# Attention with a distance bias and a channel MLP: stores from own tiles, weight casts moved to GpSimd, one load asked for sooner

## The chip, the cores and the metric

The kernel runs on one core of a Trainium2 chip. The core has a matrix engine (TensorE, PE), a vector engine (VectorE, DVE), a scalar engine (ScalarE, ACT), a general engine (GpSimd, POOL) and SyncE (SP), which here issues every DMA. Each has its own queue of instructions, run in order, and they wait for each other by semaphores. The metric is device microseconds of one execution, median of several.

## The reference

Four batches, 8 heads, 576 positions, head width 64, all in float32. Attention with a bias that depends on the distance, then a mixing over positions of rank 32, then a two-layer MLP over channels:

```python
rel = pos[:, None] - pos[None, :]
x = log1p(abs(rel)) / log1p(maximum(pos[:, None], 1))
bias = maximum(x[..., None] @ w1 + b1, 0) @ w2          # 576 x 576 x 8 heads
attn = softmax(q @ k.T / 8 + bias)                      # per batch and head
x = attn @ v                                            # heads side by side: 4 x 576 x 512
u = x + (x.T @ U @ V).T                                 # U 576 x 32, V 32 x 576
out = u + maximum(u @ w_ch1, 0) @ w_ch2                 # 512 -> 2048 -> 512
```

## The kernel before

Stage 1 computes the bias tables (a loop over 36 blocks, ACT, PE and DVE) and writes them to DRAM, from where they are loaded when a pair needs them. It already runs the first score rows of pair 0.

Then come 16 pairs. A pair is two heads of one batch, four pairs to a batch. A pair has 9 slots; `slot(p, s)` issues one block of scores (PE, L310), adds the bias (DVE, L312), takes exponentials (ACT, L331), transposes earlier blocks on PE (`tb`, `ti`, `tm`) and copies them to SBUF (`tr`, `tr_m`, `tr_mid`: "a" is a copy on ACT, L358, "d" one on DVE, L360), and multiplies with v (L414). The previous pair's output is put into `x_sb` by `assemble` (PE transposes L432 and L434, DVE scaling L437, which writes chunks 0 and 1 for the first half and chunks 2 and 3 for the second, and copy of chunk 4, L360). `x_sb` holds one batch: 128 rows by 5 chunks by 512 channels.

Products that need float32 precision are split into a high part (the value rounded by a cast) and a low part (the rest). For q and k `load_part` loads `raw` (one buffer) in two halves per pair, and `prep_ops` makes high (POOL, L142) and low parts (POOL, L150) in four steps, two of them for each half.

After a batch's four pairs its mixing runs inside the next pair, in pairs 5, 9 and 13, and for the last batch within the MLP: `mix_t`, `mix_r`, and then `mix_h` for five chunks in slots 3 (chunk 4), 4 (0 and 1) and 5 (2 and 3). `mix_h` adds a chunk of the mixing to `x_sb` in place (L482) and stores it from there to `u_dram` (L483). In these pairs the first half of the previous pair is assembled at slot 6, the second at slot 8, both into the same `x_sb`.

The MLP weights arrive as int64 words that are converted in the background. The first weight group (of four) is parked in DRAM (`wq_dram`) as float32 and loaded back by `first_weights`, which splits it into high and low parts by `split`: a cast on ACT (L567) and a subtraction on POOL (L568). This happens in pairs 13 to 15, before the MLP begins; `feed` hands it out one step per slot. The MLP then runs over 18 blocks of tokens and four weight groups (first layer L593, second L618).

The order of the work is written by hand: the loops issue the instructions in the order in which each engine will run them, and nothing reorders them. SP's queue is in order too, and a DMA that must wait for its buffer holds up the DMAs behind it.

Of the kernel before, what the change touches and what calls it, by code (L numbers as in the profile page):

```python
# [8 lines left out]
F32 = mybir.dt.float32  # L9
# [5 lines left out]
ALU = mybir.AluOpType  # L15
# [3 lines left out]
B, H, S, D = 4, 8, 576, 64  # L19
HP = H // 2  # L20
DM = H * D
# [4 lines left out]
P = 128  # L26
HALF = S // 2
LEFT = S - 4 * P
K0 = 2 * S + LEFT
QKW = 2 * K0  # L30
# [16 lines left out]
def kernel(  # L47
# [14 lines left out]
    nc = tc.nc  # L62
# [25 lines left out]
    mix = p1.enter_context(tc.tile_pool(name="mix", bufs=1, side="left"))  # L88
# [32 lines left out]
    def load_part(p, a, e):  # L121
        b, hp = divmod(p, HP)
        for lo in (0, D):
            nc.sync.dma_start(out=raw[lo : lo + D, a:e], in_=qk[b, hp, :, a:e])
# [246 lines left out]
    def tr(p, c, hd, eng):  # L371
        hf, o = q_off(c)
        pt = get_pt(p, hf)
        src = pair[p]["P"][c]
        bank = psum("t", [P, 4, P], "tb")
        b0 = 0 if hd == 0 else S + LEFT
        for kb in range(4):
            nc.tensor.transpose(bank[:, kb, :], src[:, b0 + kb * P : b0 + (kb + 1) * P], ident)  # L378
        copy(eng, pt[:, 5 * hd : 5 * hd + 4, o : o + P], bank)
# [98 lines left out]
    def mix_h(b, c):  # L478
        n = P if c < 4 else LEFT
        h = psum("t", [P, DM], "mh")  # L480
        mm(h, lhsT=v4s[:, c * P : (c + 1) * P], rhs=mixt[b], start=True, stop=True)
        nc.vector.tensor_tensor(out=x_sb[0:n, c, :], in0=h[0:n], in1=x_sb[0:n, c, :], op=ALU.add)  # L482
        nc.sync.dma_start(out=u_dram[b * S + c * P : b * S + c * P + n, :], in_=x_sb[0:n, c, :])  # L483

    NP = B * HP

    def slot(p, s):

        new, old = p < NP, p > 0
        if new and (p, s) != (1, 0):  # L490
            scores(p, s)
        if old and s == (AV_OLD if new else AV_LAST):
            av(p - 1, 1)
        if old and s == 0:
            tr(p - 1, 3, 0, "a")
        elif old and s == 1:
            tr(p - 1, 3, 1, "a")
            tr_mid(p - 1, 1, "d")
        elif old and s == (6 if p > HP and p % HP == 1 else 4):
            assemble(p - 1, 0)  # L500
        elif old and s == 8:
            assemble(p - 1, 1)
        if new and 3 <= s <= 8:
            c, hd = divmod(s - 3, 2)
            tr(p, c, hd, "a" if p % HP == 1 and 2 < s < 6 else "da"[hd])
            if s == 5:
                tr_m(p, "a")
            elif s == 6:
                tr_mid(p, 0, "d")
        if new and (p, s) != (1, 0):  # L510
            exps(p, s)
        if s > 0 and new:
            recip(p, s - 1)
        elif s == 0 and old:
            recip(p - 1, 8)
        if new and p > 0 and s == AV_NEW:
            av(p, 0)
# [46 lines left out]
    def split(g, which, k, a, e):  # L564
        def fin(y):
            h, l = (w[:, k, a:e] for w in wq[g][2 * which : 2 * which + 2])
            nc.scalar.copy(out=h, in_=y)  # L567
            nc.gpsimd.tensor_tensor(out=l, in0=y, in1=h.bitcast(F32), op=ALU.subtract)  # L568

        return fin  # L570
# [138 lines left out]
    for i in range(len(order) + 2):  # L709
        if i == 2:  # L710
            nc.vector.tensor_scalar(
                out=tab[:, CUT:NTAB], in0=tab[:, CUT:NTAB], scalar1=w1_sb, scalar2=None, op0=ALU.mult
            )
        if i < len(order):
            bias_hid(order[i])
        if i == len(order) - 1:
            nc.gpsimd.tensor_scalar(
                out=warm, in0=hids[order[i]][3][:, 0:1], scalar1=1.0, scalar2=0.0, op0=ALU.mult, op1=ALU.add
            )
        if i >= 2:  # L720
            bias_mm(order[i - 2])
            bias_out(order[i - 2])
        if i == 9:
            loads += bias_loads(4, 0)
        if i >= 16 and (i - 16) % 8 == 0:
            loads += bias_loads((i - 16) // 8, 0)
        for o in loads[:2]:
            o()
        del loads[:2]
        if 8 <= i < 12:  # L730
            prep.pop(0)()
        if i == 13:
            load_part(1, 0, QKW)
        if i in (20, 26):
            load_v({20: 0, 26: 1}[i])
        if i in early:
            slot(0, early[i])
# [23 lines left out]
    def first_weights(which):  # L761
        ys = []
        for k in range(KD + 2):
            if k < KD:
                ys.append(wrawp.tile([P, CW], I64, tag="wraw", name="y0").bitcast(F32))
                nc.sync.dma_start(out=ys[k], in_=wq_dram[4 * which + k])
            if k >= 2:
                split(0, which, k - 2, 0, DM)(ys[k - 2])
            yield

    feed = iter(())
    for p in range(NP):
        if p > 1:
            new_pair(p)
        if 0 < p < HP - 1:
            bias[p + 1] = big.tile([P, 9 * S], F32, tag=f"big{p + 1}", name=f"bias{p + 1}")
            loads = [o for c in (4, 0, 1, 2, 3) for o in bias_loads(c, p + 1)]
        for s in range(9):
            if s == (1 if p else 0) and p < NP - 1:
                prep = prep_ops(p + 1)  # L780
            if s in ((3, 4, 5, 6) if p else (0, 1, 2, 3)) and p < NP - 1:
                prep.pop(0)()
            if s == 4 and 0 < p < NP - 1:
                load_v(p + 1)
            if s in (6, 8) and 0 < p < NP - 2:
                load_part(p + 2, *((0, K0) if s == 6 else (K0, QKW)))
            if (p, s) == (CONV_FROM[0], 0):
                queue += by_twos(jobs)
                for g in range(4):
                    rows = slice(g * RANK, (g + 1) * RANK)  # L790
                    nc.vector.tensor_copy(
                        fold[rows].rearrange("p (a b) -> p a b", a=4),
                        ident[rows, rows].unsqueeze(1).to_broadcast([RANK, 4, RANK]),
                    )
            if (p, s) == (0, 7):
                av(0, 0)
                new_pair(1)
                scores(1, 0)
                exps(1, 0)
            n = 2 if p else 3  # L800
            for o in loads[0:n]:
                o()
            del loads[0:n]
            if p > 0 or s not in early.values():
                if p > HP and p % HP == 1 and s == 0:
                    mix_t(p // HP - 1)
                slot(p, s)
                conv = (0 if p > HP and p % HP == 1 else 1, 2, 6, 7, 8)
                background(int(s in conv and (p, s) >= CONV_FROM))
            if p > HP and p % HP == 1:  # L810
                if s == 2:
                    mix_r(p // HP - 1)
                for c in {3: (4,), 4: (0, 1), 5: (2, 3)}.get(s, ()):
                    mix_h(p // HP - 1, c)
            if p == NP - 3 and s == 1:
                t = big.tile([P, 9 * S], F32R, tag="big0", name="w1q")
                uth0, *wq[0] = big_views(t, [(4 * LINE, None), (UT, KD), (WQ, KD), (WQ, KD)])
                feed = first_weights(0)
            if p == NP - 2 and s == 1:
                t = big.tile([P, 9 * S], F32R, tag="big1", name="w2q")  # L820
                w2a, w2b, utl0 = big_views(t, [(WQ, KD), (WQ, KD), (UT, KD)])
                wq[0] += [w2a, w2b]
                ut[0] = [(0, uth0)], [(0, utl0)], 0
                feed = first_weights(1)
            if p == NP - 1 and s == 1:
                t = big.tile([P, 9 * S], F32, tag="big2", name="acc")
                acc.update(enumerate(big_views(t, [(DM, 0)] * 10)))
                feed = iter(())
            if p >= NP - 3 and s in (1, 2, 4, 5, 7, 8):
                next(feed, None)  # L830
            if p == NP - 1 and s in (1, 2, 3, 4, 5):
                load_acc(2 * s - 2)
                load_acc(2 * s - 1)
            if p == NP - 1 and s in (6, 7):
                if s == 7:
                    subtract()
                subtract = make_ut(0, s - 6, late=True)
# [3 lines left out]
    def run(*steps):  # L841
        for o in steps:
            o()

    m = [mlp1((0, j, None)) for j in range(3)]
    y = [mlp2((0, j, None)) for j in range(3)]
    slot(NP, 0)
    subtract()
    run(m[0][0])
    t = big.tile([P, 9 * S], F32R, tag="big3", name="ut")  # L850
# [5 lines left out]
    make_ut(1, 0)  # L856
    run(m[0][1])
    slot(NP, 1)
    run(m[0][2])
    make_ut(1, 1)  # L860
    run(m[0][3])
# [152 lines left out]
```

## Time and profile before

| | us |
|---|---|
| median of 3 runs (lowest, highest) | 743.91 (743.39, 745.29) |
| the profiled execution, its own time | 742.59 |
| its span, first to last instruction | 740.5 |
| busy in the span: PE, PEld, DVE, ACT, POOL | 720.5, 579.9, 470.7, 361.3, 241.8 |

PEld is the loading of weights into PE, beside its matmuls. A pair takes from 15.91 to 20.63 us. The page's line on PE in 40 slices of the span reads 8 or 9 tenths busy and above nearly everywhere after the first slices, and PEclk reads 9 in all 40, so that the granted clock never fell. In the rows further down a duration stands behind the start time; "[0.62 <-POOL lo L150]" says that the engine sat idle for 0.62 us before this instruction and that POOL's writing of lo at line 150 ended it. An "xN" behind a row is the number of like instructions that it sums up.

### The profile page before, as it was taken

To read this page: it belongs to the slowest core of one execution; us is meant where nothing else is said; L and a number is where in the kernel's file an instruction comes from. 1 tells how busy PE (TensorE), PEld (TensorE's weight loads), DVE (VectorE), ACT (ScalarE), POOL (GpSimd) and SP (SyncE) were. 2 spreads that over 40 slices of the span, in tenths; PEclk is the share of its full clock that TensorE was granted. 3 is DMA by queue.
4 is the path that set the end of the run, shared out by engine and by line. 5 is a ranking of instruction groups with operands and counts; after the bars stand their busy time and mean duration, and the time that the engine had idled before them with its cause. 6 is when DMAs were issued, how large, how long until landed. Compare 5 with 4: busy or idle time off the path is not lost.

```text
span 740.5 us, 12624 instructions
## 1 busy us (share of the span) xinstructions
PE 720.5 (97%) x4628; PEld 579.9 (78%) x4628; DVE 470.7 (64%) x1018; ACT 361.3 (49%) x807; POOL 241.8 (33%) x256
## 2 busy tenths in 40 slices
PE   6989999999999999999999999999999999999998
PEld 3436888778877887888788888888888888888886
DVE  7995779889978876653447655784456832333343
ACT  7997777878878777862134332440133411011010
POOL 0004567757755657800003333451024500000000
PEclk9999999999999999999999999999999999999999
DMA  7789997475555556500332121230012200001111
GB/s 219 231 306 306 279 276 166 113 204 145 162 165 158 139 139 191 180 27 1 100 135 62 53 72 57 72 100 29 1 42 78 66 0 1 1 28 58 58 42 72
DMA packets 41533, 83.93 MB, mean 113 GB/s; under 512 B 7168, under 2 KB 9856, under 8 KB 41216
## 3 DMA queue, kind: packets, MB, share of 16 engines
q1 hardware_dynamic: 41472, 83.13, 38.0%
q8 instruction: 37, 0.61, 0.4%
q14 instruction: 24, 0.20, 0.1%
HBM read 60.96 MB, written 22.15 MB: 112 GB/s over the span
## 4 chain that ended last, share of the span: by engine, by line
PE 86%; ACT 7%; DMA 3%; DVE 2%; issue 1%; POOL 0%; DVEq 0%; ACTq 0%
PE ph L593 27%; PE po L618 27%; PE o L414 11%; PE sc L310 10%; PE tb L378 7%; ACT ring L235 2%; ACT ring L257 2%; DMA u_dram<-x_sb 1%; ACT p L331 1%; DMA bias_dram<-ring 1%; PE tu L545 1%; PE ti L395 1%; PE bs L246 1%; PE tx L432 1%; PE mt L454 1%
## 5 line engine op out<-in xcount | busy, mean ns | idle before, releaser
L599 DVE SCALAR_TENSOR_TENSOR hh<-ph,hh 128x1024 fp32r<-128x1024 f32 x36 | 44.1, 1224 | 144.6 <-ACT hh L598 144.6
L598 ACT ACTIVATE hh<-ph 128x1024 fp32r<-128x1024 f32 x36 | 37.0, 1027 | 189.9 <-PE ph L593 189.9
L621 DVE TENSOR_TENSOR acc<-po,acc 128x512 f32<-128x512 f32 x132 | 88.4, 684 | 32.3 <-PE po L618 32.2
L201 POOL TENSOR_TENSOR wy<-wt,wy 128x256 int32<-128x256 int32 (+1 forms) x68 | 50.4, 742 | 179.0 <-DVE wt L196 133.5
L331 ACT ACTIVATE p<-p,st 128x576 f32<-128x576 f32 x128 | 100.0, 782 | 6.9 <-DVE st L312 5.8
L618 PE MATMUL po<-w2q,hh 128*128 128x512 f32 x432 | 102.5, 391 | 0.4 <-DVE x_sb L482 0.4
L312 DVE CUSTOM_DVE_ANT_0 p<-sc,bias 128x576 f32<-128x576 f32 x128 | 95.9, 752 | 8.5 <-PE sc L310 6.4
L618 PE MATMUL po<-wq,hh 128*128 128x512 f32 x432 | 100.7, 389 | 0.0
L310 PE MATMUL sc<-hi 128*128 128x288 f32 x320 | 99.6, 329 | 0.0
L618 PEld LDWEIGHTS po<-wq,hh 128*128 128x128 f32 x432 | 81.0, 188 | 16.8
L618 PEld LDWEIGHTS po<-w2q,hh 128*128 128x128 f32 x432 | 80.6, 188 | 17.1 <-ACT ut L548 0.6
L593 PE MATMUL ph<-ut,w1q 128*128 128x512 f32 (+1 forms) x432 | 92.8, 368 | 0.0
L310 PE MATMUL sc<-lo,hi 128*128 128x288 f32 x320 | 89.1, 295 | 0.6 <-POOL lo L150 0.6
L593 PE MATMUL ph<-ut,wq 128*128 128x512 f32 x384 | 89.6, 389 | 0.0
L414 PE MATMUL o<-pt,v 128*64 128x320 f32 (+1 forms) x640 | 85.9, 411 | 0.0
L593 PEld LDWEIGHTS ph<-ut,w1q 128*128 128x128 f32 x432 | 74.7, 188 | 13.7 <-issue 0.6
L593 PEld LDWEIGHTS ph<-ut,wq 128*128 128x128 f32 x384 | 72.1, 188 | 15.0
L378 PE MATMUL tb<-ident,p 128*128 128x128 f32 x512 | 78.1, 275 | 3.9 <-ACT wy L181 1.2
L378 PEld LDWEIGHTS tb<-ident,p 128*128 128x128 f32 x512 | 60.1, 140 | 12.3 <-issue 6.4
L414 PEld LDWEIGHTS o<-pt,v 128*64 128x64 f32 x640 | 48.0, 136 | 27.1 <-issue 3.2
L310 PEld LDWEIGHTS sc<-hi 128*128 128x128 f32 x320 | 60.4, 189 | 9.3 <-issue 3.5
L358 ACT COPY pt<-tb 128x512 f32<-128x512 f32 x88 | 51.2, 582 | 28.1 <-PE tb L378 27.8
(96 smaller groups left out, 1023.3 us busy)
## 6 DMA issues: line engine op xcount, KB each, us to landing
raw<-in_qk_dram SPq DMA_DIRECT2D x56, 304.0 KB, 5.1
wraw<-in_w_ch_dram SPq DMA_DIRECT2D x64, 256.0 KB, 2.7
bias_dram<-ring SPq DMA_DIRECT2D x36, 288.0 KB, 3.9
v<-in_vp_dram SPq DMA_DIRECT2D x16, 320.0 KB, 3.7
bias<-bias_dram SPq DMA_DIRECT2D x16, 288.0 KB, 5.0
acc<-u_dram SPq DMA_DIRECT2D x18, 256.0 KB, 4.9
out_dram<-acc SPq DMA_DIRECT2D x18, 256.0 KB, 2.0
bias<-bias_dram SPq DMA_DIRECT2D x16, 256.0 KB, 5.6
```

What stands on the lines that cost most here:

```text
L201: nc.gpsimd.tensor_tensor(out=st["y"], in0=st["t"], in1=st["y"], op=ALU.add)
L310: mm(ps[:, a, 0:HALF], lhsT=hi[:, q0 : q0 + P], rhs=kk, start=(i == 0), stop=(i == n - 1))
L312: nc.vector.tensor_tensor_reduce(out=halves(dst), in0=ps[:, :, 0:HALF], in1=halves(bias[hp][:, s * S : (s + 1) * S]), scale=-0.125, scalar ...
L331: nc.scalar.activation(out=dst, in_=dst, func=AF.Exp, bias=st[:, s : s + 1], scale=-1.0, accum_out=st[:, 10 + s : 11 + s])
L358: nc.scalar.copy(out=out, in_=in_)
L378: nc.tensor.transpose(bank[:, kb, :], src[:, b0 + kb * P : b0 + (kb + 1) * P], ident)
L414: mm(o[hd * D : (hd + 1) * D, 0:n], lhsT=v[:, vb * D : (vb + 1) * D], rhs=pt[:, pb, :], start=(j == 0), stop=(j == 4),)
L593: mm(st["ps"][:, f, :], lhsT=w, rhs=x, start=(i == 0), stop=(i == 3 * KD - 1))
L598: nc.scalar.activation(out=hh[u], in_=st["ps"], func=AF.Relu)
L599: nc.vector.scalar_tensor_tensor(out=hl[u], in0=st["ps"], scalar=0.0, in1=hh[u].bitcast(F32), op0=ALU.max, op1=ALU.subtract)
L618: mm(ps, lhsT=h, rhs=w, start=(m == 0), stop=(m == 3 * nf - 1))
L621: nc.vector.tensor_tensor(out=a, in0=ps, in1=a, op=ALU.add)
```

## The change

Five edits. First, `mix_h` writes chunks 0 and 1 into tiles of their own (u0, u1) and stores them from there; chunks 2 to 4 stay as they were. Second, in pair 1 the copies of pt in slots 3 to 5 go to DVE and ACT in turn, as in an ordinary pair, where they all went to ACT. Third, pair 1's q and k are loaded in two halves in stage 1, at blocks 13 and 17, where one load at block 13 had fetched both. Fourth, pair 4's halves are asked for in slots 4 and 6 of pair 2 instead of 6 and 8. Fifth, `first_weights` no longer uses `split`: its cast is a POOL instruction like L142, in front of POOL's subtraction. Both weight sets are now fed in pair 14 (slots 1, 2, 4, 7), pair 15 (slots 1, 2, 3, 4, 5, 7) and after the first two closing slots, where they were fed in pairs 13 to 15.

```diff
@@ mix_h
-        nc.vector.tensor_tensor(out=x_sb[0:n, c, :], in0=h[0:n], in1=x_sb[0:n, c, :], op=ALU.add)
-        nc.sync.dma_start(out=u_dram[b * S + c * P : b * S + c * P + n, :], in_=x_sb[0:n, c, :])
+        u = mix.tile([P, DM], F32, tag=f"u{c}", name="u") if c < 2 else x_sb[:, c, :]
+        nc.vector.tensor_tensor(out=u[0:n], in0=h[0:n], in1=x_sb[0:n, c, :], op=ALU.add)
+        nc.sync.dma_start(out=u_dram[b * S + c * P : b * S + c * P + n, :], in_=u[0:n])
@@ slot
-            tr(p, c, hd, "a" if p % HP == 1 and 2 < s < 6 else "da"[hd])
+            tr(p, c, hd, "a" if p > HP and p % HP == 1 and 2 < s < 6 else "da"[hd])
@@ stage 1
-        if i == 13:
-            load_part(1, 0, QKW)
+        if i in (13, 17):
+            load_part(1, *((0, K0) if i == 13 else (K0, QKW)))
@@ first_weights
-                split(0, which, k - 2, 0, DM)(ys[k - 2])
+                h, l = (w[:, k - 2] for w in wq[0][2 * which : 2 * which + 2])
+                nc.gpsimd.tensor_scalar(
+                    out=h, in0=ys[k - 2], scalar1=1.0, scalar2=0.0, op0=ALU.mult, op1=ALU.add
+                )
+                nc.gpsimd.tensor_tensor(out=l, in0=ys[k - 2], in1=h.bitcast(F32), op=ALU.subtract)
@@ the loop of the pairs
-            if s in (6, 8) and 0 < p < NP - 2:
-                load_part(p + 2, *((0, K0) if s == 6 else (K0, QKW)))
+            at = (4, 6) if p == 2 else (6, 8)
+            if s in at and 0 < p < NP - 2:
+                load_part(p + 2, *((0, K0) if s == at[0] else (K0, QKW)))
...
-                feed = first_weights(0)
...
-                feed = first_weights(1)
+                feed = (None for which in range(2) for _ in first_weights(which))
...
-                feed = iter(())
-            if p >= NP - 3 and s in (1, 2, 4, 5, 7, 8):
+            if s in {NP - 2: (1, 2, 4, 7), NP - 1: (1, 2, 3, 4, 5, 7)}.get(p, ()):
                 next(feed, None)
@@ the closing slots
     slot(NP, 0)
+    next(feed)
...
     slot(NP, 1)
+    next(feed)
```

On SP, in pair 2, slots 4 to 8, the order before is this (bias_1102 is the bias of pair 3, raw the halves of pair 4's q and k, wraw words to be converted):

```order
L129 DMA v<-in_vp_dram 128x640
L274 DMA bias_1102<-bias_dram 128x576
L274 DMA bias_1102<-bias_dram 128x512
L274 DMA bias_1102<-bias_dram 128x64
L274 DMA bias_1102<-bias_dram 128x576
L124 DMA raw<-in_qk_dram 64x1216 x2
L274 DMA bias_1102<-bias_dram 128x512
L274 DMA bias_1102<-bias_dram 128x64
L171 DMA wraw<-in_v_dram 128x256
L124 DMA raw<-in_qk_dram 64x1216 x2
```

And now, with the same bias under the name bias_1104:

```order
L129 DMA v<-in_vp_dram 128x640
L124 DMA raw<-in_qk_dram 64x1216 x2
L274 DMA bias_1104<-bias_dram 128x576
L274 DMA bias_1104<-bias_dram 128x512
L274 DMA bias_1104<-bias_dram 128x64
L274 DMA bias_1104<-bias_dram 128x576
L124 DMA raw<-in_qk_dram 64x1216 x2
L274 DMA bias_1104<-bias_dram 128x512
L274 DMA bias_1104<-bias_dram 128x64
L171 DMA wraw<-in_v_dram 128x256
```

The first half of raw has moved past four bias loads, the second past two more and past the load of wraw.

On POOL, in pair 14, from behind the pm of that pair to the pm of pair 15, before (hi and lo are pair 15's q and k, w2q the second-layer weights):

```order
L142 TENSOR_SCALAR hi<-raw 128x1216
L150 TENSOR_TENSOR hi<-raw,hi 64x608 x2
L568 TENSOR_TENSOR w2q<-y_3902,w2q 128x512
L142 TENSOR_SCALAR hi<-raw 128x1216
L568 TENSOR_TENSOR w2q<-y_3911,w2q 128x512
L150 TENSOR_TENSOR lo<-raw,hi 128x608 x2
L568 TENSOR_TENSOR w2q<-y_3965,w2q 128x512
L568 TENSOR_TENSOR w2q<-y_3991,w2q 128x512
L351 TENSOR_SCALAR pm<-praw,st 128x576
```

And now (w1q the first-layer weights, which before had their turn in pair 13 and at the start of pair 14):

```order
L142 TENSOR_SCALAR hi<-raw 128x1216
L150 TENSOR_TENSOR hi<-raw,hi 64x608 x2
L770 TENSOR_SCALAR w1q<-y_3894 128x512
L773 TENSOR_TENSOR w1q<-y_3894,w1q 128x512
L142 TENSOR_SCALAR hi<-raw 128x1216
L150 TENSOR_TENSOR lo<-raw,hi 128x608 x2
L770 TENSOR_SCALAR w1q<-y_3903 128x512
L773 TENSOR_TENSOR w1q<-y_3903,w1q 128x512
L351 TENSOR_SCALAR pm<-praw,st 128x576
```

Before the last two low parts of pair 15's k stood two subtractions, and now a cast and a subtraction; behind them there were two subtractions, now a cast and a subtraction.

On ACT, in pair 14, slots 4 to 8, before (L331 exponentials, L358 copies of transposed blocks):

```order
L358 COPY pt<-tb 128x4x128
L331 ACTIVATE p,st<-p,st 128x576
L567 CAST w2q<-y_3902 128x512
L358 COPY pt<-tm 128x4x64 x2
L331 ACTIVATE p,st<-p,st 128x576
L567 CAST w2q<-y_3911 128x512
L358 COPY pt<-tb 128x4x128
L331 ACTIVATE p,st<-p,st 128x576 x2
L567 CAST w2q<-y_3965 128x512
L358 COPY pt<-tb 128x4x128
L331 ACTIVATE p,st<-p,st 128x576
```

And now:

```order
L358 COPY pt<-tb 128x4x128
L331 ACTIVATE p,st<-p,st 128x576
L358 COPY pt<-tm 128x4x64 x2
L331 ACTIVATE p,st<-p,st 128x576
L358 COPY pt<-tb 128x4x128
L331 ACTIVATE p,st<-p,st 128x576 x2
L358 COPY pt<-tb 128x4x128
L331 ACTIVATE p,st<-p,st 128x576
```

The casts are gone, and nothing has come in their place.

## Rows read from the trace of the kernel before

**Rows 1.** The page, part 1: busy us (share of the span) xinstructions of each engine.

```profile
PE 720.5 (97%) x4628; PEld 579.9 (78%) x4628; DVE 470.7 (64%) x1018; ACT 361.3 (49%) x807; POOL 241.8 (33%) x256
```

**Rows 2.** Windows: us; busy us of PE, PEld, DVE, ACT, POOL; PEclk; DMA; GB/s.

```profile
116.65:133.47 16.82, 16.20 (x127) 13.54 (x127) 15.19 (x37) 13.36 (x36) 14.02 (x15) 1.00 0.51 133
133.47:153.72 20.25, 19.54 (x151) 14.66 (x150) 17.16 (x40) 15.03 (x38) 15.37 (x15) 1.00 0.62 168
153.72:169.63 15.91, 15.91 (x128) 13.49 (x127) 13.41 (x39) 13.11 (x34) 8.59 (x9) 1.00 0.61 159
201.44:221.89 20.45, 19.28 (x150) 14.69 (x150) 16.72 (x42) 15.21 (x38) 13.30 (x12) 1.00 0.61 175
269.65:290.28 20.63, 19.35 (x150) 14.70 (x149) 13.74 (x36) 14.57 (x36) 13.39 (x12) 1.00 0.60 181
290.28:307.02 16.74, 16.36 (x128) 13.55 (x127) 11.49 (x34) 13.96 (x35) 12.16 (x11) 1.00 0.58 150
414.78:740.50 325.72, 322.14 (x1489) 269.37 (x1487) 163.42 (x267) 71.16 (x149) 60.72 (x83) 1.00 0.14 46
```

**Rows 3.** Timeline of stage 1: start, us, engine, line, out<-in, [idle before <-releaser].

```profile
37.87 0.76 DVE L312 CUSTOM_DVE_ANT_0 p<-sc,bias 128x576 f32<-128x576 f32 x1 [0.70 <-DMA bias<-bias_dram]
...
38.67 0.78 ACT L331 ACTIVATE p<-p,st 128x576 f32<-128x576 f32 x1 [0.26 <-DVE st L312]
```

**Rows 4.** Timeline around pair 4's first scores; last row: the tile bias, 60 to 126 us.

```profile
103.75 1.08 SPq L274 DMA_DIRECT2D bias<-bias_dram  x2
...
116.42 1.21 POOL L142 TENSOR_SCALAR hi<-raw 128x1216 fp32r<-128x1216 f32 x1 [0.93 <-DMA raw<-in_qk_dram]
...
117.70 3.02 POOL L150 TENSOR_TENSOR lo<-raw,hi 128x608 fp32r<-128x608 f32 x2
...
116.72 0.75 DVE L312 CUSTOM_DVE_ANT_0 p<-sc,bias 128x576 f32<-128x576 f32 x1
...
120.78 0.40 PE L310 MATMUL sc<-lo,hi 128*128 128x288 f32 x1 [0.62 <-POOL lo L150]
...
DMA to landing us min/median/max: 2.9/5.3/8.8
```

**Rows 5.** Timeline of the mix pairs 5, 9, 13; last row: the waits of DVE.

```profile
152.37 0.44 PE L432 MATMUL tx<-ident,ot 128*128 128x128 f32 x2 [0.35 <-DVE x_sb L360]
...
153.16 0.63 PE L378 MATMUL tb<-ident,p 128*128 128x128 f32 x4 [0.35 <-DVE pt L360]
...
151.64 0.42 DVE L437 TENSOR_TENSOR x_sb<-tx,st 128x256 f32<-128x256 f32 x1 [1.22 <-DMA u_dram<-x_sb]
...
220.14 0.63 PE L378 MATMUL tb<-ident,p 128*128 128x128 f32 x4 [1.17 <-ACT wy L181]
...
288.55 0.63 PE L378 MATMUL tb<-ident,p 128*128 128x128 f32 x4 [0.98 <-DVE x_sb L360]
...
DVE x_sb L437 <- DMA u_dram<-x_sb: 3.2, 3, 1.2
```

**Rows 6.** Timeline of pair 13, ACT and PE.

```profile
283.75 0.61 ACT L567 CAST w1q<-y 128x512 fp32r<-128x512 f32 x1
...
284.90 0.51 PE L481 MATMUL mh<-ts,v4s 128*128 128x512 f32 x1 [0.30 <-ACT pt L358]
```

**Rows 7.** Timeline of pair 14, ACT and PE.

```profile
304.50 0.62 ACT L567 CAST w2q<-y 128x512 fp32r<-128x512 f32 x1
...
306.43 0.66 PE L378 MATMUL tb<-ident,p 128*128 128x128 f32 x4 [0.36 <-ACT p L331]
```

**Rows 8.** Timeline of POOL in pairs 14 and 15, and PE's first second-layer matmuls.

```profile
303.43 1.29 POOL L568 TENSOR_TENSOR w2q<-y,w2q 128x512 fp32r<-128x512 f32 x1 [1.21 <-issue]
...
307.10 2.93 POOL L150 TENSOR_TENSOR lo<-raw,hi 128x608 fp32r<-128x608 f32 x2
...
313.71 1.04 POOL L351 TENSOR_SCALAR pm<-praw,st 128x576 f32<-128x576 f32 x2 [1.19 <-DVE st L343]
...
344.59 5.64 PE L618 MATMUL po<-w2q,hh 128*128 128x512 f32 x24
```

## The prediction, made before the changed kernel was run

> **What bounds the kernel now.** I read the page's busy shares first. TensorE (PE) is busy for 720.5 of 740.5 us, 97% [rows 1]. No other engine is near that, so an edit to VectorE (DVE), ScalarE (ACT), GpSimd (POOL) or the DMA queue is worth only the time in which PE waits for it. The change alters no matmul: PE can win back idle time and nothing else.
>
> Next I read the windows [rows 2]. The granted clock is 1.00 in every one, the 2.4 GHz level, so no stage has a clock to win or lose. From 414.78 us to the end PE is busy for 322.14 of 325.72 us, and there the edits move nothing. The pairs are different. I cut them at the 20 value matmuls with which every pair begins. Pair 6 (153.72 to 169.63) is one without a wait: 15.91 us, PE busy 15.91. Against it stand pair 4 (16.82) and pair 14 (16.74) with the same matmuls. Pairs 5, 9 and 13 also carry a batch's mixing, and take 20.25, 20.45 and 20.63 us with PE busy for 19.54, 19.28 and 19.35. Their PE work is one and the same, so the smallest busy time, 19.28, is the most that such a pair can need.
>
> Last I read the timelines for what each of these waits is for. Pair 4: PE's score matmul at 120.78 sat idle 0.62 us for POOL's low parts of k, which were late because POOL's cast before them had sat 0.93 us for the DMA of raw [rows 4]. Mix pairs: PE's transposes sat idle 0.35 and 0.35 us in pair 5, 1.17 in pair 9 and 0.98 in pair 13. DVE's assembly of x_sb (L437) had sat for the store of x_sb to u_dram, three times, 3.2 us in all, 1.22 of it in pair 5 [rows 5]. The page calls the 1.17 a wait for ACT's L181; DVE's wait, of almost that size and right before it, is the cause I go by. Pair 13 loses 0.30 us more behind a copy of pt on ACT, which stood behind a weight cast of 0.61 us [rows 6]. Pair 14: 0.36 us behind an exponential on ACT, with a cast of 0.62 us shortly before it [rows 7].
>
> **The change part by part.**
>
> *Own tiles for the mixed chunks 0 and 1.* L437 at slot 6 writes x_sb[:, 0:2]. It no longer has to wait until the stores of these chunks land. Nothing is added: same five additions on DVE, same five stores on SP. Behind L437 on DVE are the copies that PE's next transposes need, so DVE's wait goes straight to PE. By the windows pair 5 gains 20.25 - 19.28 = 0.97 [rows 2]. For pair 9 the same gives 1.17, but DVE's waits in pairs 9 and 13 together are 3.2 - 1.22 = 2.0, about 1.0 each [rows 5]; I take 1.0. For pair 13 I take PE's idle time in front of this wait, 0.98. Together 2.95. Lower bound: pair 5 by its recorded idle of 0.70, and half of the rest if the next wait (chunks 2 and 3, which stay in x_sb) comes up: 1.7. Upper: 0.97 + 1.17 + 1.35 = 3.5, of which 0.3 is the next part's.
>
> *The casts leave ACT.* Eight ACT casts of about 0.61 us go, four in pair 13 and the start of 14, four in pair 14 and the start of 15. PE gains the 0.30 of pair 13 [rows 6] and, in pair 14, 16.74 - 15.91 = 0.83 [rows 2], of which only 0.36 stands in one idle row [rows 7]: the rest lies in matmuls that start a little late each. Together 1.13, bounds 0.66 and 1.2.
>
> The Trainium skill ("Perfetto Trace Analysis", Identifying the Most-Contended Engine) calls matmul busy time a poor measure of nearness to the limit, since matmuls are pipelined. This trace agrees: pair 14 shows 16.36 busy for work that takes 15.91 in pair 6 [rows 2]. By idle rows alone the change would win 4.1, by periods 5.2.
>
> POOL takes eight casts over, and before did only the subtraction, 1.29 us [rows 8]. No row shows a POOL cast of 128x512. The nearest is the same instruction over 128x1216, 1.21 us [rows 4], by elements 1.21 x 512/1216 = 0.51. Bounds: nothing below the 0.51 is in reach, and 1.21 if size did not matter; I take 0.51. The cover: in pair 14 the order is now one cast and one subtraction ahead of the low parts of pair 15's k, 0.51 + 1.29 = 1.80, where two subtractions stood, 2.58. So these low parts (307.10 before) come 0.8 us sooner; at 1.21 for the cast it is 2.50 against 2.58, still no later. POOL is busy 12.16 of 16.74 us there [rows 2], has 1.21 us idle before a subtraction, and 1.19 before the pm of pair 15 [rows 8]. After pm (over at 314.75) come six cast-and-subtract steps, 6 x 1.80 = 10.8, done by 325.6 if nothing else holds them; the second-layer weights are first read by PE at 344.59 [rows 8]. Cost to PE: 0, at either bound.
>
> The Trainium skill ("Perfetto Trace Analysis", Optimizing GPSIMD Operations) speaks against this part: other engines are to be preferred, GpSimd being slower in general. Per element these rows show the reverse for this cast, 0.51 against 0.62, as an estimate. By the rule the work would take longer, and whether anything waits for it is the third rival.
>
> *Pair 4's q and k asked for two slots sooner.* A slot is 15.91/9 = 1.77 us, so both halves are asked for 3.5 us sooner; POOL's wait was 0.93. POOL's low parts ended at 117.70 + 3.02 = 120.72 and would now end at 119.79; PE would want them at 120.78 - 0.62 = 120.16 [rows 4]. The stall goes, 0.4 us to spare. By the windows 16.82 - 15.91 = 0.91, by the idle row 0.62; I take 0.91. The price lies on SP, which issues in order: the last bias loads of pair 3 are now behind both halves. They were issued at 103.75, landing 2.9 to 8.8 us after issue, and DVE uses the bias at 116.72. Two more issues cost about 1.08, as two do there; 104.83 + 8.8 = 113.6 leaves 3.1 us for the extra bytes ahead. I take no cost; if the bytes took longer, DVE would wait up to the 0.91 gained.
>
> *Pair 1.* Its load in two halves at i = 13 and 17 puts half of the bytes in front of stage 1's bias loads. DVE sat 0.70 us for one of these, and ACT 0.26 for DVE [rows 3]. ACT sets the pace in stage 1, so 0.26 is the gain, bounds -0.3 (the second half now holds a later bias load as long) and 0.26. Two copies of pt per pair 1 go from ACT to DVE; I see no row in which PE idles for them and take 0, bounds -0.2 and 0.2.
>
> Sum: 2.95 + 1.13 + 0.91 + 0.26 = 5.25 us. The profiled execution took 742.59 (span 740.5 and 2.09 around it), which would become 737.3. The median of the runs shown is 743.91, 1.32 higher, and goes to 738.7. Every part of it lies ahead of 414.78, and from there on PE is the bound, so what PE gains it keeps.
>
> **The rivals.**
>
> *The next wait takes over.* In the mix pairs DVE is busy for 17.16 of 20.25 and 16.72 of 20.45 us [rows 2]; with its wait gone it has 2 to 3 us left, and the second half of x_sb still waits for stores of its own. And pair 3's bias may eat pair 4's gain. For it: the densest DVE windows of all the pairs are these. Against it: pair 13 with 13.74 busy shows the same loss as the other two, so it is the wait and not DVE's load. Then half of 2.95 and the 0.91 are lost, 2.4 in all: 741.1.
>
> *The transfers were hidden anyway.* The waits at u_dram and raw go, but PE is as late for another reason (a PSUM bank, ACT's L181, which the page names for the 1.17). Then only ACT's relief and stage 1 are left, 1.13 + 0.26 = 1.4: 742.5. Against it: idle times and waits agree in size in four places.
>
> *POOL becomes the bound, and the kernel slower.* Let a POOL cast take c. The low parts of pair 15's k are ahead of its own scores; they would be late by (c + 1.29) - 2.58 = c - 1.29, at the most, and PE with them. After pm the six steps take 6(c + 1.29), and 344.59 - 314.75 = 29.84 us are there, so from c = 3.7 on PE waits for the second-layer weights too, with 6 us for each us of c. The gain is used up at (c - 1.29) + 6(c - 3.7) = 5.25, so c = 4.1; at c = 4.5 the kernel takes 743.91 - 5.25 + 3.2 + 4.8 = 746.7. For it speaks that no row shows this shape on POOL; against it that the same instruction over 2.4 times the elements takes 1.21.
>
> **How the numbers follow.** The forecast, about 738.7, has a chance of 0.68; its own range is 738.1 to 740.1: at the upper bounds 3.5 + 0.9 + 0.91 + 0.46 = 5.8 is gained, and by idle rows alone 4.1, less 0.3 if stage 1 loses, 3.8. The next wait takes over: 0.18, at about 741.1. Hidden anyway: 0.10, at 742.5. POOL the bound: 0.04, at 746.7. About 0.3%, 2.2 us, is what a measurement of this kernel can tell from no change, so faster means below 741.7. Faster: all of the forecast and of the first rival, 0.86. Same: 0.10. Slower: 0.04. The range, 737.0 to 741.4, takes in the forecast with its bounds, 1.1 below it for the spread of the runs, which is 743.39 to 745.29 now, and most of the first rival; about 0.18 is left out.
>
> **What would show it.** DVE's wait of L437 for the store of u_dram is gone in all three mix pairs, and these take 19.3 to 19.6 us. Pair 4 takes 15.9, PE has no wait for POOL's lo near 120 us, and DVE none for a bias of pair 3 near 116. No cast of w1q or w2q is on ACT before the weights of the second group, and pair 14 takes 15.9. POOL's cast of 128x512 takes about 0.5 us. I am wrong where the mix pairs stay at 20 us with the wait gone, where DVE shows a new wait for bias, or where PE waits for POOL at the first lines of the MLP (L594, L619 of the changed kernel).

## The result, and the profile after

The changed kernel takes 738.29 us (median of 5, 736.59 to 740.56); the kernel before, timed beside it, 744.61 (743.39 to 745.94). The ratio is 0.9914 with a 95% interval of 0.9887 to 0.994. The prediction was 738.7, within 737.0 to 741.4. The profiled execution took 736.59, its span is 734.8 against 740.5.

The page's first part, and the windows cut at the same places as [rows 2], with pairs 3 and 15 in addition (us; busy us of PE, PEld, DVE, ACT, POOL; PEclk; DMA share; GB/s):

```profile
PE 719.6 (98%) x4628; PEld 580.4 (79%) x4628; DVE 471.5 (64%) x1020; ACT 356.3 (48%) x797; POOL 246.8 (34%) x264
```

```profile
99.86:115.75 15.89, 15.89 (x127) 13.35 (x127) 13.48 (x37) 12.04 (x31) 9.97 (x11) 1.00 1.06 267
115.75:131.90 16.15, 16.15 (x127) 13.50 (x127) 14.53 (x37) 14.12 (x38) 13.36 (x15) 1.00 0.63 154
131.90:151.03 19.13, 19.13 (x151) 14.68 (x150) 17.30 (x42) 15.08 (x39) 15.33 (x15) 1.00 0.59 170
151.03:166.95 15.92, 15.92 (x127) 13.56 (x126) 13.17 (x37) 13.05 (x34) 8.64 (x10) 1.00 0.67 168
198.75:218.12 19.37, 19.30 (x151) 14.70 (x150) 16.64 (x42) 14.95 (x38) 13.35 (x12) 1.00 0.61 173
265.88:285.26 19.38, 19.31 (x151) 14.72 (x150) 13.58 (x36) 13.65 (x34) 11.81 (x10) 1.00 0.47 136
285.26:301.18 15.92, 15.92 (x127) 13.56 (x127) 10.74 (x31) 11.75 (x30) 8.87 (x9) 1.00 0.58 154
301.18:318.72 17.54, 17.21 (x136) 14.18 (x135) 12.00 (x35) 13.05 (x33) 14.33 (x16) 1.00 0.65 214
409.00:734.80 325.80, 322.04 (x1489) 269.27 (x1487) 163.28 (x267) 71.14 (x148) 60.55 (x83) 1.00 0.14 46
```

From above: pair 3 takes 15.89 us, at a DMA share of 1.06; pair 4 16.15 (16.82 before), pair 5 19.13 (20.25), pair 6 15.92 (15.91), pair 9 19.37 (20.45), pair 13 19.38 (20.63), pair 14 15.92 (16.74), pair 15 17.54, as before. PE's busy time has hardly changed, 719.6 against 720.5: 5.7 us of span went, nearly all of it idle time or time in which matmuls started late. The last window is as long as before, 325.80 against 325.72.

All waits of PE that the view still lists (us in all, times, the longest):

```profile
PE bs L246 <- ACT ring L235: 7.3, 6, 5.3
PE bs L246 <- ACT ring L257: 1.1, 1, 1.1
PE tb L378 <- ACT p L331: 0.8, 1, 0.8
PE po L619 <- DVE x_sb L483: 0.4, 1, 0.4
PE tx L432 <- DVE pt L360: 0.2, 1, 0.2
PE tb L378 <- DVE w2q L554: 0.2, 1, 0.2
```

Of the PE waits in [rows 4 to 7] none is left. DVE's wait for the store, 3.2 us in three times before [rows 5], now stands once:

```profile
DVE x_sb L437 <- DMA u_dram<-x_sb: 0.2, 1, 0.2
```

Not everything that stood in front of them went as forecast. This is the timeline around pair 4's first scores, which answers to [rows 4]:

```profile
103.73 0.30 PE L310 MATMUL sc<-lo,hi 128*128 128x288 f32 x1
...
104.16 0.76 DVE L312 CUSTOM_DVE_ANT_0 praw<-sc,bias 128x576 f32<-128x576 f32 x1 [1.74 <-DMA v<-in_vp_dram]
...
114.88 1.21 POOL L142 TENSOR_SCALAR hi<-raw 128x1216 fp32r<-128x1216 f32 x1 [0.97 <-DMA raw<-in_qk_dram]
...
116.17 3.01 POOL L150 TENSOR_TENSOR lo<-raw,hi 128x608 fp32r<-128x608 f32 x2
...
116.21 0.45 ACT L178 ACTIVATE wt<-wraw 128x256 f32<-128x256 f32 x1 [1.16 <-DMA wraw<-in_v_dram]
...
119.23 0.40 PE L310 MATMUL sc<-lo,hi 128*128 128x288 f32 x1
```

POOL still waits 0.97 us for raw, and ACT has a new wait of 1.16 for words of in_v. PE's row at 119.23 bears no wait: POOL ended at 119.18, just in time.

DVE's 1.74 at 104.16, in front of its row for pair 3's first scores, looks like a new DMA wait, but the name misleads. The last of the score matmuls that this row reads starts at 103.73, 0.43 us earlier. In the kernel before, the same row stands 0.43 us behind the same matmul (104.64), and there the wait is put down to PE:

```profile
105.07 0.76 DVE L312 CUSTOM_DVE_ANT_0 praw<-sc,bias 128x576 f32<-128x576 f32 x1 [2.40 <-PE sc L310]
```

It is 0.43 us in all fourteen profiles of this document, so the wait is for PE's scores in each. The bias that the row reads was asked for ahead of raw, in slot 0 of pair 2.

POOL in pairs 14 and 15, and PE's first second-layer matmuls, which answer to [rows 8]:

```profile
297.31 0.62 POOL L770 TENSOR_SCALAR w1q<-y 128x512 fp32r<-128x512 f32 x1
...
298.01 1.29 POOL L773 TENSOR_TENSOR w1q<-y,w1q 128x512 fp32r<-128x512 f32 x1
...
300.55 2.95 POOL L150 TENSOR_TENSOR lo<-raw,hi 128x608 fp32r<-128x608 f32 x2
...
319.70 1.28 POOL L773 TENSOR_TENSOR w2q<-y,w2q 128x512 fp32r<-128x512 f32 x1
...
338.75 5.64 PE L619 MATMUL po<-w2q,hh 128*128 128x512 f32 x24
```

A cast lasts 0.62 us, and its subtraction starts 0.70 us after the cast's start. The last split ends at 320.98, almost 18 us before its first reader.

### The profile page after: what moved, and what is told of

Same layout as the page of the kernel before. It is cut to its first block, busy times and chain, and to the rows that moved or that the text cites. A ratio compares the mean times of both kernels' runs of the same rounds, so it can differ in the third digit from the quotient of the medians.

```text
span 734.8 us, 12632 instructions
## 1 busy us (share of the span) xinstructions
PE 719.6 (98%) x4628; PEld 580.4 (79%) x4628; DVE 471.5 (64%) x1020; ACT 356.3 (48%) x797; POOL 246.8 (34%) x264
## 4 chain that ended last, share of the span: by engine, by line
PE 91%; ACT 5%; issue 2%; DVE 1%; DMA 0%; ACTq 0%; DVEq 0%
PE ph L594 27%; PE po L619 27%; PE sc L310 11%; PE o L414 11%; PE tb L378 8%; ACT ring L235 2%; PE bs L246 1%; ACT ring L257 1%; PE tm L386 1%; PE tx L432 1%; PE ti L395 1%; PE tu L546 1%; PE mh L481 1%; PE mt L454 1%; ACT p L331 1%
## 5 line engine op out<-in xcount | busy, mean ns | idle before, releaser
L331 ACT ACTIVATE p<-p,st 128x576 f32<-128x576 f32 x128 | 100.0, 782 | 4.1 <-DVE st L312 2.9
L358 ACT COPY pt<-tb 128x512 f32<-128x512 f32 x86 | 49.9, 581 | 28.6 <-PE tb L378 28.3
```

Source lines behind the costliest of these rows:

```text
L331: nc.scalar.activation(out=dst, in_=dst, func=AF.Exp, bias=st[:, s : s + 1], scale=-1.0, accum_out=st[:, 10 + s : 11 + s])
L358: nc.scalar.copy(out=out, in_=in_)
```

## The experiments

In all of them a pair is cut at the first of its 20 value matmuls, as in [rows 2]; "pairs 3 and 4" is the time from pair 3's cut to pair 5's, "stage 1" the time up to pair 1's cut (64.47 us before, 63.83 after).

**1. The own tiles alone.** On the kernel before:

```diff
+        u = mix.tile([P, DM], F32, tag=f"u{c}", name="u") if c < 2 else x_sb[:, c, :]
-        nc.vector.tensor_tensor(out=x_sb[0:n, c, :], in0=h[0:n], in1=x_sb[0:n, c, :], op=ALU.add)
+        nc.vector.tensor_tensor(out=u[0:n], in0=h[0:n], in1=x_sb[0:n, c, :], op=ALU.add)
```

> The kernel before with the own tiles for mixed chunks 0 and 1 alone. Theory A (each edit takes away a PE wait of its own, and the gains add up): DVE's wait of L437 for u_dram goes in all three mix pairs; pair 5 falls from 20.25 to about 19.15 us, pair 9 from 20.45 to 19.4, pair 13 from 20.63 to about 19.65 (its 0.30 behind the ACT cast stays); all other pairs as before; about 3.1 us less in all. Theory B (the gain of the mix pairs needs the other edits, since ACT's casts or a later wait would take over): half of that or less, pair 13 above 20.1.

Ratio 0.9958 (0.994 to 0.9976), median 740.52. Windows of pairs 5, 9 and 13:

```profile
134.85:153.99 19.14, 19.14 (x150) 14.69 (x149) 17.27 (x42) 15.11 (x39) 15.33 (x15) 1.00 0.59 169
201.73:221.10 19.37, 19.28 (x151) 14.69 (x150) 16.64 (x42) 15.23 (x38) 13.33 (x12) 1.00 0.59 175
268.86:288.43 19.57, 19.26 (x151) 14.68 (x150) 13.65 (x36) 14.58 (x36) 12.37 (x11) 1.00 0.59 170
```

The mix pairs gain 1.11, 1.08 and 1.06 us, 3.25 in all, without any other edit: theory A. In the three profiles of experiments 2 to 4, which lack this edit, they take 20.08 to 20.24, 20.40 to 20.53 and 20.51 to 20.61 us, so the gain is clear of what differs between executions. One thing was not expected: pair 4, in which nothing was changed, takes 18.32 us instead of 16.82.

**2. The split on GpSimd alone.** The edits to `first_weights` and to the feed's times, on the kernel before.

> The kernel before with the first MLP weights split on GpSimd in pairs 14 and 15 alone. Theory A: pair 14 falls from 16.74 to 15.92 us and pair 13 from 20.63 to about 20.33; pair 15 stays at 17.54; 1.1 us less in all. Theory B: in pair 13 the wait for the store of x_sb comes last, so ACT's 0.30 us there is hidden behind it: pair 13 stays within 0.1 of 20.63, and 0.8 us less in all.

Ratio 0.9985 (0.9957 to 1.0012), median 743.38. Pairs 13 and 14:

```profile
270.22:290.73 20.51, 19.27 (x150) 14.68 (x150) 13.66 (x36) 13.66 (x34) 11.85 (x10) 1.00 0.50 146
290.73:306.66 15.93, 15.93 (x128) 13.59 (x127) 10.68 (x31) 11.78 (x30) 8.89 (x9) 1.00 0.49 133
```

Pair 14 falls by the 0.81 us. Pair 13, at 20.51, stays within 0.12 of before (it takes 20.53 in experiment 4, which doesn't touch it): theory B. ACT's 0.30 us [rows 6] is hidden behind the store while that is waited for. With the own tiles, pair 13 goes from 19.57 (experiment 1) to 19.38, so the two together give 0.19 more.

**3. Pair 4's load alone.**

```diff
+            at = (4, 6) if p == 2 else (6, 8)
-            if s in (6, 8) and 0 < p < NP - 2:
-                load_part(p + 2, *((0, K0) if s == 6 else (K0, QKW)))
+            if s in at and 0 < p < NP - 2:
+                load_part(p + 2, *((0, K0) if s == at[0] else (K0, QKW)))
```

> The kernel before with pair 4's q and k asked for two slots sooner, alone. Theory A: pair 4 falls from 16.82 to about 16.15 us, as in the changed kernel, with 0.7 us less in all, and DVE gets a wait of 1 to 2 us for pair 3's bias near 104 us that PE does not feel. Theory B (the DMA queue is full there, and the load lands no sooner; what moved pair 4 in the changed kernel was the shift of the work before it): pair 4 stays above 16.6.

Ratio 1.0007 (0.9989 to 1.0025), median 744.34: no gain shows. Pair 4 took 17.45 us. Two rows of DVE and ACT in pair 4:

```profile
118.67 0.76 DVE L312 CUSTOM_DVE_ANT_0 p<-sc,bias 128x576 f32<-128x576 f32 x1 [0.55 <-DMA bias<-bias_dram]
...
120.13 0.45 ACT L178 ACTIVATE wt<-wraw 128x256 f32<-128x256 f32 x1 [2.84 <-DMA wraw<-in_v_dram]
```

ACT stands 2.84 us for words that were asked for behind raw, DVE 0.55 for the last part of pair 3's bias. The price that the prediction set at nothing is there. The wait near 104 us that theory A speaks of is the misread one: here that row, at 106.39, waits 2.17 us for PE's scores.

**4. Stage 1 and pair 1 alone.** The load of pair 1 in halves and the shared copies.

> The kernel before with pair 1's load in two halves and pair 1's copies shared with DVE, alone. Theory A: stage 1, up to the first value matmul of pair 1 at 64.47 us, ends 0.26 us sooner by the load (64.2), the rest of the 0.64 us seen in the changed kernel being a start that differs from run to run (PE's second group at 18.82 against 18.40); pair 1 falls from 20.39 to about 20.11 by the copies; 0.5 us less in all. Theory B: all of the 0.64 comes from the load: 63.85, with PE's second group at 18.8.

Ratio 0.9985 (0.9963 to 1.0007), median 742.11. Pair 1 and pair 4:

```profile
63.79:83.90 20.11, 19.25 (x144) 15.16 (x143) 12.32 (x37) 13.69 (x35) 10.97 (x10) 1.00 1.01 265
```

Pair 4, not edited here, is another draw: 17.65. Pair 1 falls from 20.39 to 20.11. It does so in every profile with these two edits (20.10 to 20.13, one of 20.48) and in none without them (20.37 to 20.39). That is 0.27 us; I put it down to the copies, since the load was issued by 34 us and POOL takes it up at 59 without a wait, but no run separates the two.

Stage 1 ended at 63.79, as in theory B. Over all profiles it ended at 63.75 to 64.79 with the edit (ten) and at 64.34, 64.45, 64.47 and 65.82 without (four): its start differs too much to compare ends. DVE's wait for a bias in stage 1 stands in all four (0.64 to 1.68 us) and in none of the ten. What it is worth can be read from a row of PE just before it, which every profile has, and PE's next wait behind it. In the kernel before:

```profile
35.25 1.18 PE L246 MATMUL bs<-ring,small_sb 128*32 128x288 f32 x16 [0.68 <-ACT ring L235]
...
41.79 2.47 PE L246 MATMUL bs<-ring,small_sb 128*32 128x288 f32 x32 [1.42 <-ACT ring L257]
```

And in the changed kernel:

```profile
34.97 1.18 PE L246 MATMUL bs<-ring,small_sb 128*32 128x288 f32 x16 [0.68 <-ACT ring L235]
...
41.14 2.47 PE L246 MATMUL bs<-ring,small_sb 128*32 128x288 f32 x32 [1.05 <-ACT ring L257]
```

From the start of the first of these rows to pair 1's cut pass 28.84 to 28.87 us in all ten profiles with the edit, and 29.16, 29.20 and 29.22 in three without it. The load in halves is worth 0.34 us, and the rest of the 0.64 is the start: theory A. The fourth without it has 30.46, with a slower clock (last section).

**5. The casts back on ACT, at the new times.**

```diff
-                nc.gpsimd.tensor_scalar(out=h, in0=ys[k - 2], scalar1=1.0, scalar2=0.0, ...)
-                nc.gpsimd.tensor_tensor(out=l, in0=ys[k - 2], in1=h.bitcast(F32), op=ALU.subtract)
+                split(0, which, k - 2, 0, DM)(ys[k - 2])
```

> The changed kernel, but with the casts of the first MLP weights left on ACT at their new times (pairs 14 and 15, closing slots). Theory A (what helps is that ACT is relieved): pair 13 stays at 19.4 us, since nothing is cast there any more; pair 14 takes 16.2 to 16.7 instead of 15.92, pair 15 17.8 to 18.4 instead of 17.54; 0.5 to 1.5 us more than the changed kernel. Theory B (what helps is the new time alone): pair 14 at 15.92, pair 15 at 17.54. Pair 4, which has the sooner load here, gives one more sample of it: 16.2 to 17.5.

Ratio 0.9922 (0.9894 to 0.995), median 738.73. Pairs 14 and 15:

```profile
285.64:301.86 16.22, 16.20 (x128) 13.54 (x127) 11.04 (x32) 12.38 (x32) 8.14 (x8) 1.00 0.55 144
301.86:319.50 17.64, 17.25 (x135) 14.18 (x135) 11.78 (x34) 14.78 (x38) 8.64 (x9) 1.00 0.66 210
```

Against the changed kernel 0.30 and 0.10 us, 0.4 in all. Moving the work out of pair 13 and thinning it out in pair 14 gives most of the gain (0.6 of the 1.0 us that pairs 13 to 15 win beside the own tiles), taking it off ACT the rest. Both theories hold a part.

**6. GpSimd's casts at the old times.** The feed as before, the casts as in the changed kernel.

> The changed kernel, but with the first MLP weights fed at the old times (pairs 13 to 15), cast on GpSimd. Theory A (the new times are needed because GpSimd would be too late for pair 15's k): two cast-and-subtract steps of 0.70 + 1.28 stand ahead of pair 15's low parts, these end near 305.4 us where PE wants them near 304.25, so pair 15 takes 18.5 instead of 17.54, with a PE wait for POOL; pairs 13 and 14 as in the changed kernel. Theory B (GpSimd has room enough anyway): all pairs as in the changed kernel. Pair 4: 16.2 to 17.5.

Ratio 0.9921 (0.9898 to 0.9944), median 739.27. Pair 15 takes 18.47 us, with this row of PE:

```profile
305.93 0.40 PE L310 MATMUL sc<-lo,hi 128*128 128x288 f32 x1 [0.64 <-POOL lo L150]
```

As theory A had it, 18.5: two splits ahead of pair 15's low parts are one too many.

**7. Every GpSimd cast four times over.**

```diff
+                for _ in range(4):
                     nc.gpsimd.tensor_scalar(...)
```

> The changed kernel with each GpSimd cast of the first MLP weights made four times over (same result), so that a cast costs about 2.8 us instead of 0.70. Theory A (the sum of the third rival): pair 15's low parts end 2.1 us later, at 305.6, against 0.75 us of slack, so pair 15 takes 18.9 instead of 17.54 with a PE wait for POOL; the first and second layers of the MLP wait for nothing; 1.3 us more in all. Theory B (GpSimd's work is covered more deeply, or less): pair 15 within 0.3 of 17.54, or over 20, or a wait for POOL at the first lines of the MLP. Pair 4: 16.2 to 17.5.

Ratio 0.9928 (0.9903 to 0.9952), median 739.69. Pair 15 takes 18.75 us instead of 17.54, with one wait for POOL, and the MLP waits for nothing:

```profile
310.62 0.40 PE L310 MATMUL sc<-lo,hi 128*128 128x288 f32 x1 [0.90 <-POOL lo L150]
```

1.21 us against 1.35 worked out. The third rival's own sum gives 2.8 - 1.29 = 1.5 us "at the most", and that holds: a cast of 2.8 us costs 1.21 here, and the kernel would still have been faster. Pairs 3 and 4 took 36.55 us, with the same instructions as the changed kernel's 32.04.

**8. The changed kernel without pair 4's sooner load.** The edit of experiment 3 undone.

> The changed kernel without the sooner load of pair 4's q and k. Theory A (the load is worth 0.7 us on the average, under a spread of about 1 us that the DMA queue brings): pair 4 takes 16.8 to 18.3 us as in the four profiles without the sooner load so far (16.82, 18.32, 17.34, 17.65). Theory B (the load is worth nothing; pair 4 is short when the DMAs of pairs 1 to 3 happen to land early): pair 4 within 16.1 to 17.5. A single profile tells little here; it is read together with the other three of this set, which have the sooner load.

Ratio 0.9937 (0.9912 to 0.9961), median 740.03 (738.39 to 744.44). Pair 4 took 19.61 us. All profiles together, but for experiments 10 to 12, which change more: pairs 3 and 4 took 32.70, 33.24, 34.02, 34.22 and 36.15 us without the sooner load, 31.83, 32.04, 32.41, 33.34, 35.50 and 36.55 with it. The means, 34.07 and 33.61, are closer than the spread. The medians speak for the load (740.03 against 738.29 and, below, 738.25), but come from different runs. What this edit is worth stays open.

What it shifts is clearer. PE's listed waits for POOL's low parts in these pairs sum to 0, 0, 0.3, 0.3, 1.7 and 2.6 us with the sooner load, and to 0.6, 1.0, 1.4, 1.9 and 2.0 without. ACT's first conversion of the words behind raw starts after 1.16 to 4.77 us of idle time in all six with it, and without a wait in all five without it. DVE waits for the last part of pair 3's bias in three of the six (0.55, 2.14 and 3.10 us) and in none of the five.

**9. The changed kernel once more.** The same program.

> The changed kernel once more, for a second profile of the same program and more times. Theory A (the spread of pairs 3 and 4 is the DMA queue's and differs from execution to execution): everything from pair 5 on as in the first profile within 0.1 us a pair, pairs 3 and 4 together anywhere between 31.8 and 36.5 us, stage 1 between 63.7 and 64.7. Theory B (the first profile's 32.04 is the program's own): within 0.3 of it. The ratio to the kernel before about 0.992.

Ratio 0.9905 (0.9889 to 0.9921), median 738.25 (736.66 to 741.08). The profiled execution is the longest of the six, 741.08. From pair 5 on every pair is within 0.02 us of the first profile. Pair 4 takes 19.37 us against 16.15, pairs 3 and 4 35.50 against 32.04: theory A.

Rows of POOL, DVE and PE in pair 4:

```profile
118.19 1.21 POOL L142 TENSOR_SCALAR hi<-raw 128x1216 fp32r<-128x1216 f32 x1 [3.06 <-DMA raw<-in_qk_dram]
...
120.21 0.76 DVE L312 CUSTOM_DVE_ANT_0 p<-sc,bias 128x576 f32<-128x576 f32 x1 [3.10 <-DMA bias<-bias_dram]
...
121.03 0.40 PE L310 MATMUL sc<-lo,hi 128*128 128x288 f32 x1 [0.82 <-POOL lo L150]
...
122.48 0.40 PE L310 MATMUL sc<-lo,hi 128*128 128x288 f32 x1 [0.91 <-POOL lo L150]
```

POOL waits 3.06 us for raw, 0.97 in the first profile; DVE 3.10 for the bias.

**10. The load of pair 4 left out.** Pair 4 computes with old contents of raw.

```diff
-            if s in at and 0 < p < NP - 2:
+            if s in at and 0 < p < NP - 2 and p != 2:
```

> The changed kernel with the loads of pair 4's q and k left out (the old contents of raw are used, so pair 4 computes something else). Theory A (pair 4's stall is raw landing late): pairs 3 and 4 together take 31.8 us (2 x 15.9), with no PE wait for POOL. Theory B (the whole DMA queue of pairs 1 to 3 is late, so that bias and the words of in_v are late too): PE waits for POOL go, waits of ACT or DVE for a DMA of 0.5 us and more stay, and pairs 3 and 4 may take more than 32.2.

Ratio 0.989 (0.9878 to 0.9903), median 736.97 (736.78 to 737.23). Pairs 3 and 4:

```profile
100.40:116.29 15.89, 15.89 (x127) 13.58 (x127) 13.13 (x37) 12.73 (x34) 10.48 (x12) 1.00 0.66 205
116.29:132.21 15.92, 15.92 (x127) 13.56 (x126) 14.37 (x37) 13.37 (x36) 12.48 (x14) 1.00 0.45 125
```

31.81 us together, no PE wait for POOL. One DVE wait of 2.0 us keeps the name of a DMA, but it is the misread one, for PE's scores; ACT waits for no words. So theory A. The spread of the times shrinks from 4.4 us (six runs of experiment 9) to 0.45 (four runs): most of what differs from execution to execution is when the bytes of pair 4 and those behind them land, and it costs the changed kernel 1.3 us at the median.

**11. The loads of pairs 2, 3 and 4 left out.** These pairs compute with old contents.

> The changed kernel with the loads of q and k left out for pairs 2, 3 and 4 (old contents are used; these pairs compute something else), 3.6 MB less in pairs 1 to 3. Theory A (bytes: the queue is full there, and all that is late is late behind bytes): the DMA share of these pairs falls from about 1.0 to 0.8 or less, no engine waits for bias, v or words, pairs 2, 3 and 4 take 15.9 each. Theory B (something else than bytes, such as the order of issue on SP, makes the landings late): DVE or ACT still waits a microsecond or more for bias or for the words of in_v.

Ratio 0.9888 (0.9876 to 0.9901), median 736.88 (736.55 to 737.03). Pair 3:

```profile
100.28:116.17 15.89, 15.89 (x127) 13.34 (x126) 12.49 (x37) 12.74 (x34) 8.97 (x11) 1.00 0.22 57
```

The DMA share of pair 3 falls from 1.06 in the changed kernel to 0.22, and all DMA waits of pairs 2 to 4 go: theory A, it is bytes. That it is no faster than experiment 10 says that with pair 4's load out the other two no longer reach PE.

**12. The conversion begun three slots later**, as an attempt at a better version.

```diff
-                background(int(s in conv and (p, s) >= CONV_FROM))
+                background(int(s in conv and (p, s) >= (3, 1)))
```

> The changed kernel with the background conversion of the weights begun three slots later (slot 1 of pair 3 instead of slot 6 of pair 2), so that ACT and DVE come to the words of in_v later than the full DMA queue of pairs 1 to 3 brings them. Theory A (what is left of the stall of pairs 3 and 4 is ACT's wait for these words, 1.2 us in the changed kernel and 2.8 to 4.4 us where the queue is slower): that wait goes, and pairs 3 and 4 together take 31.8 to 32.3 us at any pace of the queue; up to 1 us faster than the changed kernel. Theory B (they wait for raw and bias as well): 32 to 34 us still.

Ratio 0.9976 (0.9961 to 0.9991), median 742.98: slower than the changed kernel. Pair 5:

```profile
132.90:154.83 21.93, 20.90 (x150) 15.14 (x149) 17.07 (x44) 15.57 (x39) 15.88 (x16) 1.00 0.47 138
```

ACT's wait for the words is gone, and pairs 3 and 4 take 32.20 us (16.29 of it pair 4), as theory A has it, though in one profile. But pair 5 takes 21.93 us instead of 19.13, pair 9 20.96 instead of 19.37, pair 13 19.95 instead of 19.38: PE gets new waits for DVE there (0.9 us for ts, 0.4 for x_sb in the view of waits). That the steps of the conversion now fall otherwise on the mix pairs is the likely cause; no run tests it. The gain is paid back there.

## Why the prediction was right, and where it was not

**Right in the main term.** DVE's wait for the store was the cause of PE's idle time in the mix pairs, the 1.17 that the page put down to L181 [rows 5] included. It was taken at 2.95 us; alone it measured 3.25, by the same windows (experiment 1). The next wait did not take over. Two deductions (1.0 for pair 9, 0.98 for pair 13) were too careful: PE's lateness is more than what DVE's row calls its wait.

**Right in pair 14, with one term counted that was not free-standing.** 0.83 was forecast and 0.81 measured. The 0.30 of pair 13 [rows 6] is worth nothing that shows alone and 0.19 with the own tiles. Experiment 5 adds that the new times do more than the engine: left on ACT, the casts cost PE 0.4 us in pairs 14 and 15.

The rule of the Trainium skill on matmul busy time ("Perfetto Trace Analysis", Identifying the Most-Contended Engine) proved useful in pair 14: the trace after shows 15.92 busy where 16.36 stood before for the same matmuls, and the 0.81 gained is what the periods said, over twice the 0.36 of the idle row [rows 7]. The page's reason is that pipelined matmuls look smaller in a trace; what differs here is that the same matmuls, started late, read longer.

**Right that POOL has room, wrong in the price.** Between the bounds 0.51 and 1.21 the cast takes 0.62, or 0.70 from start to start; the scaling by elements was a little low, the margin large. So POOL is not quicker at this cast than ACT, as the prediction had estimated, but as quick (0.61 to 0.62 on ACT [rows 6 and 7]). The low parts of pair 15's k came 1.5 us sooner, counted from pair 14's cut (15.29 us behind it against 16.82), where 0.8 was worked out. Experiments 6 and 7 show where it ends: one split more ahead of pair 15's low parts costs 0.93 us.

**Wrong in how pair 4's load would land.** The prediction has both halves asked for 3.5 us sooner, so that the stall goes with "0.4 us to spare", and takes no cost. Both steps failed. In the first profile POOL's cast behind the load came 1.54 us sooner (114.88 against 116.42), and 0.90 of that is that the pair as a whole began sooner (115.75 against 116.65). The DMA share is 1.06 in the stretch before it, and what raw wins there is taken from the words and at times from the bias (experiment 8). The stall of 0.91 us, taken for the program's own, belonged to one execution: with the same instructions up to there, experiments 1 and 2 show pair 4 at 18.32 and 17.34 us, and the changed kernel's own instructions give 15.94 (experiment 6) to 19.37 (experiment 9). One profile could not tell this.

**Stage 1 right, a little low.** 0.26 was forecast, as the upper bound too, and 0.34 measured (experiment 4).

**Wrong to take pair 1's copies at nothing.** No idle row of PE stood there, yet the pair's period fell by 0.27, just beyond the bound of 0.2.

**The total was partly luck.** The median moved by 6.3 us, where 5.25 was forecast. The parts that repeat from profile to profile give 3.25 + 0.81 + 0.19 + 0.27 + 0.34 = 4.86, and the prediction had 2.95 + 1.13 + 0.26 = 4.34 for them. The rest, 1.5, lies in pairs 3 and 4 and in the start of stage 1, which differ from execution to execution; that it is near the 0.91 forecast for pair 4 shows nothing, since the interval of the ratio, times the 744.61 of before, reaches from 4.5 to 8.4 us.

## What to carry to other kernels

Where a buffer is both changed in place and stored, look whether its next writer waits for the store to land; a tile of its own for the stored value took that wait away here, and it was worth the difference of periods and not only the idle row. Before a load is asked for sooner, look at the DMA share of the stretch: at 1.0 to 1.06, as here, what the load gained others waited for. Where a view names a DMA as the end of a wait, compare the row with the end of the other work that it needs: DVE's row here stood 0.43 us behind PE's last score matmul under five different names (PE, issue, and the landings of v, bias and raw). And where a stretch hangs on landings, one profile of it is one draw: take the cut times of several executions before a stall of a microsecond is booked as a gain. Where starts differ, count from a row that all executions share.

## What the hardware showed that was not expected

A short stall of PE can cost more than itself. In the profile of experiment 8 PE had idled for 0.64 and 0.98 us in pair 4, and then the granted clock fell from 1.00 to 0.50 (the 1.2 GHz level of the two) for about 3 us, while PE was busy all the time. Windows of it (PEclk is the third number from the right; the first row holds the first stall and the start of the second, the second row its end):

```profile
117.07:122.00 4.93, 3.77 (x24) 1.82 (x23) 3.94 (x6) 3.42 (x10) 3.81 (x3) 1.00 0.82 183
122.00:123.00 1.00, 0.54 (x4) 0.54 (x5) 0.00 (x0) 0.00 (x0) 0.92 (x2) 1.00 0.02 8
123.00:124.00 1.00, 1.00 (x8) 1.00 (x8) 0.57 (x1) 0.00 (x0) 0.94 (x2) 0.76 0.40 68
124.00:125.00 1.00, 1.00 (x7) 0.98 (x6) 0.31 (x3) 0.96 (x2) 0.00 (x0) 0.50 0.98 302
125.00:126.00 1.00, 1.00 (x7) 1.00 (x5) 0.77 (x2) 0.83 (x4) 0.00 (x0) 0.50 0.98 233
126.00:127.00 1.00, 1.00 (x7) 1.00 (x6) 0.71 (x3) 1.00 (x2) 0.02 (x1) 0.54 0.11 20
```

At half clock two us of matmuls do the work of one: 0.24 + 0.50 + 0.50 + 0.46 = 1.7 us of pair 4's 19.61 are lost in that way; from 127 on, with PE busy since 123, the clock is at 1.00 again. In the profile of experiment 3 the same stands in stage 1, behind the idle time of this row of PE, with DVE's wait of 1.68 us for a bias before it; the clock was 0.78 and 0.88 on the average of the windows 41 to 46 and 46 to 51 us, and stage 1 ended at 65.82 us, the latest of all:

```profile
42.88 7.83 PE L246 MATMUL bs<-ring,small_sb 128*32 128x288 f32 x96 [2.13 <-ACT ring L257]
```

In the other executions with similar stalls (the second of the changed kernel, with 0.82 and 0.91 us) the clock stayed at 1.00. So a late landing is not only a wait; in two of fourteen profiles the clock fell behind one. Why in these and not in the others stays open.
